# A first pair split by columns over two queues, and the first batch's natural keys of pairs 2 and 3 loaded instead of turned

## The chip, the core and the metric

The kernel runs on one core of a Trainium2 chip. The time is the device time of one execution in microseconds (us), from launch to end, median over the runs shown. The core has five engines with instruction streams of their own: PE (TensorE, matmuls), DVE (VectorE), ACT (ScalarE), POOL (GpSimd) and SP (SyncE, which here only issues transfers). Each works through its stream in order; PE alone fetches weights ahead. SP and ACT both issue direct transfers (DMAs), each on a queue of its own, and the same 16 DMA engines serve both queues.

## The reference

Inputs q, k, v are 8 batches x 8 heads x 576 positions x 64; the mixture of experts has 8 experts of 512 x 1024 x 512.

```python
scores = scale * np.matmul(q, k.transpose(0, 1, 3, 2))
rel = pos[:, None] - pos[None, :]
Dmat = np.where(rel >= 0, gamma[:, None, None] ** rel[None, :, :], 0.0)
ret = np.matmul(scores * Dmat[None], v)            # retention, no softmax
x = ret.transpose(0, 2, 1, 3).reshape(4608, 512)   # one row per token
...
expert_idx = np.argmax(logits, axis=1)             # one expert per token
h = np.maximum(x[mask] @ w1[e], 0.0)
out[mask] = gate_w[mask, None] * (h @ w2[e])
```

## The kernel before, in words

**Attention.** A batch is worked on in four pairs of heads (p = 0 to 3) and four chunks of 128 positions, with a tail of 64. For a pair the host lays q and k out turned (`qk`, head dimension on the partitions, 2 x 576 columns), k once more naturally (`kn`, positions on the partitions), and v naturally. Per batch: `emit_A` multiplies k by q within each chunk (8 matmuls per pair, each two pieces in the trace) and DVE multiplies the two result banks by the decay matrix into `raw`. `emit_U` (for the first batch `emit_U0`, two pairs at a time) multiplies natural k, scaled by a power of gamma, with v and sums over the chunks into the state `Tst`: ACT copies chunk 0, DVE adds the other three. `emit_O` adds scores times v, `emit_S` adds the state times q, `emit_At` and `emit_Ot` do the tail. The rows then go to DRAM (`xd`), and routing runs beside it. After batch 7 the mixture of experts takes from about 140 us to the end.

**The first batch** stands apart (`first_batch`), since it runs while its data arrive. `keep_warm` gives PE 38 dummy matmuls of 132 columns. Natural k of batch 0 isn't loaded: for each pair `turn_k` transposes four chunks of k on PE into one bank, and DVE scales that bank into `kt` (line 699). The order on PE: dummies, A and turn of pair 0, a small product for the experts' norms (`norm_E`), A and turn of pair 1, `emit_O(0, 0)`, `emit_U0(0)`, then A and turn of pair 2, A and turn of pair 3, `emit_S(0, 0)`, `emit_At`, `emit_U0(1)`, `emit_O(0, 1)`, `emit_S(0, 1)`, `emit_Ot`. POOL builds decay matrices and scales q. From batch 1 on POOL scales loaded k (`scale_k`, line 689). PSUM has eight banks; in the first batch `psa` hands out four in turn (a_64 to a_67 in the rows) and `psm` the other four.

**Order of the work.** All five streams are written in program order (`tc.manual_schedule`). A DMA takes one of eight semaphores (DMAHW0 to DMAHW7) in turn, over both queues together; so the ninth DMA isn't issued until the DMA that last held its semaphore has landed, and an engine that issues DMAs stands still at that point. On ACT this matters for more than DMAs: all of ACT's first transfers stand ahead of its first computation, the copy of `Tst` chunk 0 (line 775), which needs the activation table loaded just before it. Transfers of batch 0, in program order: `cs` (constants; SP), pair 0 as rows 0 to 95 of q (SP), k (ACT), rows 96 to 127 of q (ACT), pair 1 as q (SP) and k (ACT), the second constants (ACT), the first half of v (both), pairs 2 and 3 (q on SP, k on ACT), the second half of v (both), the tail constants `decayt` and `gtail` (ACT), the tail of v (SP). Then SP goes on with batch 1: four times 576 KB of `qk`, 1024 KB of `kn`, 1152 KB of v.

Of the kernel before, what the change touches and what calls it, by code (L numbers as in the profile page):

```python
# [9 lines left out]
F32 = mybir.dt.float32  # L10
# [33 lines left out]
SECOND = (0, 4, 1, 5, 2, 3, 6, 7)  # L44
BIG = 1.0e6
NWARM = 38
WWARM = 132
NO = NT + 2
NVS = 4

# [45 lines left out]
def retention_moe(ctx: ExitStack, tc: tile.TileContext, qk, kn, v0s, vs, w1, w2, head, cst, out):  # L96
# [38 lines left out]
    def cc(name):  # L135
        if name == "iota":
            return iota
        o, w = _C[name]
        return cs[:, o : o + w] if o < _FIRST else late["cd"][:, o - _FIRST : o - _FIRST + w]
# [364 lines left out]
    with ExitStack() as att:  # L504
# [16 lines left out]
            return lambda: on.tensor_tensor(out=lo, in0=raw, in1=hi.bitcast(F32), op=ALU.subtract)  # L521

        both = (nc.sync, nc.scalar)

        def load_qk(b, p):
            t = qkp.tile([P, 2, S], F32, name="qkt")
            if b == 0:
                n = 96 if p == 0 else P
                for i, on in enumerate(both):
                    m = P if i else n  # L530
                    on.dma_start(out=t[:m, i], in_=qk[b, p, :m, i])
                if n < P:
                    nc.scalar.dma_start(out=t[n:, 0], in_=qk[b, p, n:, 0])
            else:
                nc.sync.dma_start(out=t, in_=qk[b, p])
            qkt[b, p] = t
# [20 lines left out]
        def load_decay(o, w, on=nc.sync):  # L557
            on.dma_start(out=cd[:, o : o + w], in_=cst[:, o : o + w])
# [14 lines left out]
            on.dma_start(out=v0[:, c, : DM // 2], in_=v1[:, c, : DM // 2])  # L573
        load_qk(0, 2)
        load_qk(0, 3)
        for i, on in enumerate(both):
            c = slice(2 * i, 2 * i + 2)
            on.dma_start(out=v0[:, c, DM // 2 :], in_=v1[:, c, DM // 2 :])
        load_decay(0, _C["decayt"][1] + _C["gtail"][1], nc.scalar)
        nc.sync.dma_start(out=vt_[0][:, KW:], in_=v0s[:, KW:])  # L580
        kt[0] = a1.tile([P, KW], F32, name="kt", bufs=2)

        onef = ap.tile([P, P], F32, name="onef")
        part = cc("part")
# [91 lines left out]
        def kview(b):  # L676
            return kt[b].rearrange("p (c n) -> p c n", c=NCH)
# [15 lines left out]
        def turn_k(p):  # L693

            ps = psa.tile([P, 512], F32, name="a")
            for c in range(NCH):
                nc.tensor.transpose(ps[:, c * P : (c + 1) * P], qkt[0, p][:, 1, c * P : (c + 1) * P], ident)
            g = cc("gneg").rearrange("p (c h) -> p c h", c=NCH)[:, :, 2 * p : 2 * p + 2]
            nc.vector.tensor_tensor(
                out=kview(0)[:, :, p * P : (p + 1) * P].rearrange("p c (h d) -> p c h d", h=2),  # L700
                in0=ps.rearrange("p (c h d) -> p c h d", c=NCH, h=2),
                in1=g.unsqueeze(3).broadcast_to([P, NCH, 2, D]),
                op=ALU.mult,
            )

        def scale_q(b, p):
            q = qkt[b, p][:, 0, P : NCH * P]
# [232 lines left out]
        def first_batch():  # L940
            build_decay(0)
            square_E()
            emit_A(0, 0)
            turn_k(0)
            norm_E()
            build_decay(1)
            build_g(0)
            emit_A(0, 1)
            turn_k(1)
            build_decay(2)  # L950
            scale_q(0, 0)
            build_decay(3)
            build_g(1)
            scale_q(0, 1)
            build_g(2)
            build_g(3)
            emit_O(0, 0)
            emit_U0(0)
            for p in (2, 3):
                emit_A(0, p)  # L960
                turn_k(p)
                scale_q(0, p)
            emit_S(0, 0)
            emit_At(0)
            build_rest()
            emit_U0(1)
            emit_O(0, 1)
            build_E()
            scale_k(1)
            emit_S(0, 1)  # L970
            emit_Ot(0)
# [626 lines left out]
```

## Time and profile before

| | |
|---|---|
| median of 3 runs | 570.05 us (569.20 to 570.09) |
| the profiled execution's own time | 570.68 us |
| its span, first to last instruction | 568.7 us |
| PE busy | 560.5 us, 99% of the span |
| DVE, ACT, POOL busy | 420.7, 384.6, 235.2 us |
| DMA engines' mean busy share from 5 to 120 us | about 1.0 |
| chain that ended last, by engine | PE 80%, DMA 11%, waits for issue 3%, DVE 2%, ACT 2% |

A row of the timeline gives the start, the length, engine, line and operation, the tiles (output <- input) and how many were merged; in brackets the idle time before it and what ended it. A row of the chain gives the start, the length without overlap, and what the chain ran through. "L697" is line 697 of the kernel before.

### The profile page before, as it was taken

The page shows a single profiled execution, that of the slowest core. Times are in us where ns is not written, and L with a number is a line of the kernel's source. Part 1 is how long each engine was busy: PE and PEld are TensorE (multiplying, and loading weights), DVE is VectorE, ACT ScalarE, POOL GpSimd, SP SyncE. Part 2 cuts the span into 40 slices and gives each one's busy share as a digit, 9 for nine tenths or more (in the row PEclk, how much of TensorE's full clock was granted, in tenths as well). Part 3 has the DMA queues.
Part 4 walks back from the last instruction along what each step waited for, and adds up shares of the span by engine and source line. Part 5 has one row for each costly group of instructions (what it writes and reads, how often), then busy time and mean ns, then how long its engine had stood idle before and what let it go on. Part 6 is the DMA issues. An engine that isn't in the chain of part 4 may idle for free.

```text
span 568.7 us, 13084 instructions
## 1 busy us (share of the span) xinstructions
PE 560.5 (99%) x5090; PEld 508.5 (89%) x5090; DVE 420.7 (74%) x938; ACT 384.6 (68%) x700; POOL 235.2 (41%) x233
## 2 busy tenths in 40 slices
PE   8999999999999999999999999999999999999996
PEld 8898999888998899889989988998899899889986
DVE  3756768889866868877887878688778778786810
ACT  0156455457759887987787788778877877867611
POOL 6673534563446740562075126405520650242012
PEclk9999999999999999999999999999999999999999
DMA  9999999967469573557448445735564584432201
GB/s 300 406 368 373 376 342 350 389 204 242 169 207 181 180 200 116 156 160 181 124 142 196 139 117 189 182 112 168 164 150 131 158 185 143 138 99 85 75 37 50
DMA packets 74832, 109.22 MB, mean 192 GB/s; under 512 B 42344, under 2 KB 43788, under 8 KB 73872
## 3 DMA queue, kind: packets, MB, share of 16 engines
q1 hardware_dynamic: 65616, 86.17, 49.2%
q0 software_dynamic: 7696, 19.95, 10.9%
q10 hardware_dynamic: 1456, 2.24, 1.2%
q8 instruction: 41, 0.67, 0.5%
q14 instruction: 23, 0.19, 0.1%
HBM read 80.27 MB, written 19.94 MB: 176 GB/s over the span
## 4 chain that ended last, share of the span: by engine, by line
PE 80%; DMA 11%; issue 3%; DVE 2%; ACT 2%; POOL 1%; POOLq 0%; SPq 0%; DVEq 0%; ACTq 0%
PE m L1275 19%; PE a L1207 15%; PE m L1207 11%; PE a L1275 10%; DMA out<-y,sid 9%; PE a L718 4%; PE a L459 2%; PE a L801 2%; PE m L801 2%; PE m L718 2%; PE m L459 2%; PE m L884 1%; PE a L884 1%; PE m L745 1%; DMA raw<-w 1%
## 5 line engine op out<-in xcount | busy, mean ns | idle before, releaser
L1275 PE MATMUL m<-w2s,hs 128*128 128x512 f32 x600 | 138.8, 389 | 0.0
L1275 PEld LDWEIGHTS m<-w2s,hs 128*128 128x128 f32 x600 | 112.2, 188 | 22.9
L1251 POOL DMA_INDIRECT out<-y,sid x41 | 46.6, 1136 | 193.5 <-DVE wsum L1129 125.7
L1275 PE MATMUL a<-w2s,hs 128*128 128x512 f32 (+1 forms) x384 | 83.6, 376 | 0.0
L1275 PEld LDWEIGHTS a<-w2s,hs 128*128 128x128 f32 x384 | 68.9, 188 | 13.1
L1207 PE MATMUL a<-xsb,w0s 128*128 128x320 f32 x342 | 58.0, 309 | 0.0
L1207 PEld LDWEIGHTS a<-xsb,w0s 128*128 128x128 f32 x342 | 52.1, 188 | 0.0
L362 POOL DMA_INDIRECT raw<-xd,gid x40 | 43.5, 1087 | 20.3 <-DVE sid L352 7.9
L1178 ACT ACTIVATE hs<-y 128x320 fp32r<-128x320 f32 x84 | 39.3, 474 | 17.6 <-DVE y L1219 16.7
L375 POOL DMA_INDIRECT gt<-gd,gid x40 | 43.1, 1078 | 18.9 <-issue 10.5
L1171 DVE SCALAR_TENSOR_TENSOR hs<-y,hs 128x320 fp32r<-128x320 f32 x84 | 46.7, 569 | 2.0
L410 ACT COPY raw<-raw 128x1024 uint16<-128x1024 uint16 x35 | 47.4, 1355 | 0.0
L445 ACT CAST xsb<-raw 128x128 fp32r<-128x128 f32 x70 | 32.1, 459 | 21.9 <-DVE raw L428 21.4
L689 POOL TENSOR_TENSOR kt<-kt,cs 128x512 f32<-128x512 f32 x28 | 28.3, 1042 | 43.9 <-DMA kt<-kn 43.9
L1106 DVE TENSOR_TENSOR w2s<-raw,w2s 128x1024 fp32r<-128x1024 f32 x32 | 39.1, 1222 | 7.0 <-ACT w2s L1103 6.9
L1219 DVE TENSOR_TENSOR y<-a,y 128x320 f32<-128x320 f32 x47 | 22.7, 488 | 19.8 <-ACT y L1223 13.5
L403 ACT COPY raw<-raw 128x1024 uint16<-128x1024 uint16 x35 | 35.4, 1046 | 0.0
L1103 ACT CAST w2s<-raw 128x1024 fp32r<-128x1024 f32 x32 | 33.5, 1046 | 2.6 <-DMA raw<-w 2.6
L1207 PE MATMUL m<-xsb,w0s 128*128 128x320 f32 x198 | 34.1, 309 | 0.0
L708 POOL TENSOR_TENSOR qkt<-qkt,gsb 128x384 f32<-128x384 f32 x32 | 31.3, 1003 | 6.8 <-issue 4.6
L421 DVE TENSOR_TENSOR raw<-raw 128x256 f32<-128x256 f32 x35 | 14.9, 424 | 25.7 <-ACT raw L410 25.7
L1223 ACT COPY y<-a 128x320 f32<-128x320 f32 x48 | 20.5, 427 | 16.8 <-PE a L1207 12.7
(256 smaller groups left out, 1205.2 us busy)
## 6 DMA issues: line engine op xcount, KB each, us to landing
raw<-w SPq DMA_DIRECT2D x64, 512.0 KB, 3.9
qkt<-qk SPq DMA_DIRECT2D x28, 576.0 KB, 7.5
xd<-y SPq DMA_DIRECT2D x36, 256.0 KB, 9.6
vt<-vs SPq DMA_DIRECT2D x7, 1152.0 KB, 13.0
kt<-kn SPq DMA_DIRECT2D x7, 1024.0 KB, 10.4
qkt<-qk ACTq DMA_DIRECT2D x4, 288.0 KB, 5.0
qkt<-qk SPq DMA_DIRECT2D x3, 288.0 KB, 5.7
out<-y,sid POOLq DMA_INDIRECT x41, 3.2
```

Of the source, the lines that this page charges most:

```text
L362: nc.gpsimd.indirect_dma_start(out=t[:, XO : XO + DM], out_offset=None, in_=xd[:rows, :], in_offset=bass.IndirectOffsetOnAxis(ap=gid[:, a ...
L375: nc.gpsimd.indirect_dma_start(out=g[:, i : i + 1], out_offset=None, in_=gd[:, :], in_offset=bass.IndirectOffsetOnAxis(ap=gid[:, a : a + 1 ...
L403: nc.scalar.copy(far.rearrange("p (h n) -> p h n", h=2), near.rearrange("p (n h) -> p h n", h=2))
L410: nc.scalar.copy(far.bitcast(U16).rearrange("p (n h) -> p h n", h=2), near.rearrange("p (h n) -> p h n", h=2))
L718: nc.tensor.matmul(ps[h][:, c * P : (c + 1) * P], t[hs, 1, c * P : (c + 1) * P], t[hs, 0, c * P : (c + 1) * P], start=True, stop=True,)
L1103: nc.scalar.copy(hi, u)
L1106: nc.vector.tensor_tensor(out=lo, in0=u, in1=hi.bitcast(F32), op=ALU.subtract)
L1171: nc.vector.scalar_tensor_tensor(out=lo, in0=part(src), scalar=0.0, in1=hi.bitcast(F32), op0=ALU.max, op1=ALU.subtract)
L1178: nc.scalar.activation(hi, part(src), AF.Relu)
L1207: nc.tensor.matmul(ps[:, :HC], w[:, ws, ka, d * P : (d + 1) * P], xop(kx, xsp)[:, d, :], start=(n in (1, 2, 5) and d == 0 and k == 0), sto ...
L1251: put = nc.gpsimd.indirect_dma_start(out=out.rearrange("t (k n) -> (t k) n", k=k), out_offset=bass.IndirectOffsetOnAxis(ap=rows, axis=0), ...
L1275: nc.tensor.matmul(ps[:, :step], hs[:, hsp, f, i * P : (i + 1) * P], w[:, ws, f, n : n + step], start=(j == 0 and k == 0), stop=(j == NF - ...
```

## The change

- Pair 0 of batch 0 is loaded by columns instead of by rows: columns 0 to 255 of q (SP) and of k (ACT), then 256 to 511 of k (ACT), 256 to 415 of q (SP), 416 to 511 of q (ACT). Its tail columns 512 to 575 come later, in two transfers (128 partitions x 256 B each), behind the second half of v.
- `turn_k(2)` and `turn_k(3)` are gone: eight transposes on PE and two scalings on DVE. In their place natural k of pairs 2 and 3 is loaded, 256 KB on SP (chunks 0, 1) and 256 KB on ACT (chunks 2, 3), ahead of the second half of v; pair 2 is then scaled in place by eight ACT operations of 128 x 64, pair 3 by one DVE operation of 128 x 512.
- The dummy matmuls have 112 columns instead of 132.

```diff
@@ -44,7 +44,7 @@
 SECOND = (0, 4, 1, 5, 2, 3, 6, 7)
 BIG = 1.0e6
 NWARM = 38
-WWARM = 132
+WWARM = 112
 NO = NT + 2
 NVS = 4
 
@@ -521,16 +521,17 @@
             return lambda: on.tensor_tensor(out=lo, in0=raw, in1=hi.bitcast(F32), op=ALU.subtract)
 
         both = (nc.sync, nc.scalar)
+        FIRST = ((0, 0, 0, 256), (1, 1, 0, 256), (1, 1, 256, 512), (0, 0, 256, 416), (1, 0, 416, 512))
 
         def load_qk(b, p):
             t = qkp.tile([P, 2, S], F32, name="qkt")
             if b == 0:
-                n = 96 if p == 0 else P
-                for i, on in enumerate(both):
-                    m = P if i else n
-                    on.dma_start(out=t[:m, i], in_=qk[b, p, :m, i])
-                if n < P:
-                    nc.scalar.dma_start(out=t[n:, 0], in_=qk[b, p, n:, 0])
+                if p == 0:
+                    for on, i, j, k in FIRST:
+                        both[on].dma_start(out=t[:, i, j:k], in_=qk[b, p, :, i, j:k])
+                else:
+                    for i, on in enumerate(both):
+                        on.dma_start(out=t[:, i], in_=qk[b, p, :, i])
             else:
                 nc.sync.dma_start(out=t, in_=qk[b, p])
             qkt[b, p] = t
@@ -573,12 +574,18 @@
             on.dma_start(out=v0[:, c, : DM // 2], in_=v1[:, c, : DM // 2])
         load_qk(0, 2)
         load_qk(0, 3)
+        kt[0] = a1.tile([P, KW], F32, name="kt", bufs=2)
+        k0, k1 = (x.rearrange("p (c n) -> p c n", c=NCH) for x in (kt[0], kn[0]))
+        for i, on in enumerate(both):
+            c = slice(2 * i, 2 * i + 2)
+            on.dma_start(out=k0[:, c, DM // 2 :], in_=k1[:, c, DM // 2 :])
         for i, on in enumerate(both):
             c = slice(2 * i, 2 * i + 2)
             on.dma_start(out=v0[:, c, DM // 2 :], in_=v1[:, c, DM // 2 :])
+        for i, on in enumerate(both):
+            on.dma_start(out=qkt[0, 0][:, i, NCH * P :], in_=qk[0, 0, :, i, NCH * P :])
         load_decay(0, _C["decayt"][1] + _C["gtail"][1], nc.scalar)
         nc.sync.dma_start(out=vt_[0][:, KW:], in_=v0s[:, KW:])
-        kt[0] = a1.tile([P, KW], F32, name="kt", bufs=2)
 
         onef = ap.tile([P, P], F32, name="onef")
         part = cc("part")
@@ -702,6 +709,18 @@
                 in1=g.unsqueeze(3).broadcast_to([P, NCH, 2, D]),
                 op=ALU.mult,
             )
+
+        def scale_k0(p):
+            x = kview(0)[:, :, p * P : (p + 1) * P].rearrange("p c (h d) -> p c h d", h=2)
+            g = cc("gneg").rearrange("p (c h) -> p c h", c=NCH)[:, :, 2 * p : 2 * p + 2]
+            if p == 2:
+                for c in range(NCH):
+                    for h in range(2):
+                        nc.scalar.activation(x[:, c, h], x[:, c, h], AF.Copy, scale=g[:, c, h : h + 1])
+            else:
+                nc.vector.tensor_tensor(
+                    out=x, in0=x, in1=g.unsqueeze(3).broadcast_to([P, NCH, 2, D]), op=ALU.mult
+                )
 
         def scale_q(b, p):
             q = qkt[b, p][:, 0, P : NCH * P]
@@ -958,7 +977,7 @@
             emit_U0(0)
             for p in (2, 3):
                 emit_A(0, p)
-                turn_k(p)
+                scale_k0(p)
                 scale_q(0, p)
             emit_S(0, 0)
             emit_At(0)
```

Three places of the instruction streams follow, as built. Names: `qkt` is a pair's turned q and k, `cd` the constants, `vt` v, `kt` natural k; "waits DMAHW7" means that the instruction waits until the DMA that last took semaphore 7 has landed.

ACT from its fourth transfer to the work behind the first copy, before (L531 loads k of pairs 2 and 3, the last `cd` holds `decayt` and `gtail`):

```order
L558 DMA cd<-cst 128x388
L573 DMA vt<-v0s 128x2x256 [waits DMAHW1_49]
L531 DMA qkt<-qk 128x576 [waits DMAHW3_49]
L531 DMA qkt<-qk 128x576 [waits DMAHW5_49]
L578 DMA vt<-v0s 128x2x256 [waits DMAHW7_49]
L558 DMA cd<-cst 128x512 [waits DMAHW1_49]
L775 ACT_TABLE_LOAD
L775 COPY Tst<-m_68 128x128 [waits PE_49]
L827 COPY xT<-m_70 128x512 [waits PE_49]
```

The same place in the changed kernel:

```order
L574 DMA vt<-v0s 128x2x256 [waits DMAHW2_49]
L534 DMA qkt<-qk 128x576 [waits DMAHW4_49]
L534 DMA qkt<-qk 128x576 [waits DMAHW6_49]
L581 DMA kt<-kn 128x2x256 [waits DMAHW0_49]
L584 DMA vt<-v0s 128x2x256 [waits DMAHW2_49]
L586 DMA qkt<-qk 128x64 [waits DMAHW5_49]
L559 DMA cd<-cst 128x512 [waits DMAHW7_49]
L794 ACT_TABLE_LOAD
L794 COPY Tst<-m_68 128x128 [waits PE_49]
L719 ACTIVATE kt<-kt,cs 128x64 [waits DMAHW1_49]
L719 ACTIVATE kt<-kt,cs 128x64 x3
L719 ACTIVATE kt<-kt,cs 128x64 [waits DMAHW0_49]
```

Two more transfers stand ahead of the table load there, and the last `cd`, which took over semaphore 1 from the first half of v, now takes over semaphore 7.

SP from the q of pair 1 on, before and then changed (the fourth row of the second piece is the q of pair 3):

```order
L531 DMA qkt<-qk 128x576
L573 DMA vt<-v0s 128x2x256
L531 DMA qkt<-qk 128x576 [waits DMAHW0_49]
L531 DMA qkt<-qk 128x576 [waits DMAHW2_49]
L578 DMA vt<-v0s 128x2x256 [waits DMAHW4_49]
```

```order
L534 DMA qkt<-qk 128x576
L574 DMA vt<-v0s 128x2x256 [waits DMAHW1_49]
L534 DMA qkt<-qk 128x576 [waits DMAHW3_49]
L534 DMA qkt<-qk 128x576 [waits DMAHW5_49]
L581 DMA kt<-kn 128x2x256 [waits DMAHW7_49]
```

SP's half of the new `kt` has the place that its second half of v had; it takes semaphore 7 over from the q of pair 1, and ACT's last `cd` takes it over from this `kt`.

PE from the end of batch 0's tail (`emit_Ot`) to the first scores of batch 1, before and then changed:

```order
L857 MATMUL a_66<-qkt,Tst 64x64 [waits DVE_49]
L857 MATMUL a_66<-qkt,Tst 64x64
L857 MATMUL a_67<-qkt,Tst 64x64 x2
L718 MATMUL a_64<-qkt 128x128 [waits DMAHW0_49]
L718 MATMUL a_65<-qkt 128x128
```

```order
L876 MATMUL a_64<-qkt,Tst 64x64 [waits DVE_49]
L876 MATMUL a_64<-qkt,Tst 64x64
L876 MATMUL a_65<-qkt,Tst 64x64 x2
L737 MATMUL a_64<-qkt 128x128 [waits DMAHW6_49,DVE_49]
L737 MATMUL a_65<-qkt 128x128 [waits DVE_49]
```

Two banks fewer are handed out in the first batch, so batch 1's first scores now take the two banks that the tail has just written, and wait for DVE to empty them.

## Rows read from the trace of the kernel before

**Rows 1.** The page, part 1: engine, busy us (share of the span), instructions.

```profile
PE 560.5 (99%) x5090; PEld 508.5 (89%) x5090; DVE 420.7 (74%) x938; ACT 384.6 (68%) x700; POOL 235.2 (41%) x233
```

**Rows 2.** The chain of work from 0 to 120 us: start us, us, what.

```profile
1.18 4.52 DMA qkt<-qk
5.83 2.08 PE a L718 x16
...
14.10 1.09 PE a L718 x16
15.19 0.59 PE a L697 x4
...
17.20 0.58 PE a L697 x4
...
19.05 1.08 PE a L767 x32
...
23.16 0.42 PE a L718 x4
23.82 1.83 PE a L718 x28
```

**Rows 3.** Timeline of PE, 0 to 31 us.

```profile
0.75 4.34 PE L597 MATMUL m<-const-bfloat16-1.0 128*128 128x132 bf16 x38 [0.75 <-PEq L1589]
...
12.96 1.14 PE L767 MATMUL m<-vt,kt 128*64 128x64 f32 x32
...
30.70 2.08 PE L745 MATMUL m<-vt,kt 128*64 128x64 f32 x64
```

**Rows 4.** Timeline of ACT, 0 to 30 us.

```profile
9.97 0.33 ACTq L558 DMA_DIRECT2D cd<-cst  x1
10.33 1.28 ACT L775 ACT_TABLE_LOAD   x1 [10.33 <-DMA qkt<-qk]
14.15 0.27 ACT L775 COPY Tst<-m 128x128 f32<-128x128 f32 x1 [2.54 <-PE m L767]
```

**Rows 5.** Timeline of DVE, 13 to 25 us.

```profile
14.45 0.94 DVE L777 TENSOR_TENSOR Tst<-m,Tst 128x128 f32<-128x128 f32 x3 [1.82 <-ACT Tst L775]
15.31 1.28 DVE L727 TENSOR_TENSOR raw<-a,decay 128x512 f32<-128x512 f32 x2
16.51 0.68 DVE L699 TENSOR_TENSOR kt<-a,cs 128x512 f32<-128x512 f32 x1
17.11 1.28 DVE L727 TENSOR_TENSOR raw<-a,decay 128x512 f32<-128x512 f32 x2
18.31 0.68 DVE L699 TENSOR_TENSOR kt<-a,cs 128x512 f32<-128x512 f32 x1
...
23.20 0.49 DVE L868 TENSOR_TENSOR xC<-a,cd 128x128 f32<-128x128 f32 x2 [0.97 <-PE a L857]
```

**Rows 6.** Timeline of SP, 0 to 30 us: issues of q of pair 3, v, v of batch 1.

```profile
5.71 0.33 SPq L531 DMA_DIRECT2D qkt<-qk  x1
...
7.40 0.38 SPq L578 DMA_DIRECT2D vt<-v0s  x1
...
15.55 0.46 SPq L548 DMA_DIRECT2D vt<-vs  x1
```

**Rows 7.** DMA issues near 1.2, 4.7, 5.7, 7.4, 10.0, 15.5 us: KB, us to landing.

```profile
qkt<-qk SPq DMA_DIRECT2D x1, 216.0 KB, 4.5
...
vt<-v0s ACTq DMA_DIRECT2D x1, 256.0 KB, 5.2
...
qkt<-qk SPq DMA_DIRECT2D x1, 288.0 KB, 5.8
...
vt<-v0s SPq DMA_DIRECT2D x1, 256.0 KB, 6.1
...
cd<-cst ACTq DMA_DIRECT2D x1, 256.0 KB, 8.0
...
vt<-vs SPq DMA_DIRECT2D x1, 1152.0 KB, 11.9
```

**Rows 8.** Timeline of POOL, 22 us on: the scaling of batch 1's natural k.

```profile
24.46 4.05 POOL L689 TENSOR_TENSOR kt<-kt,cs 128x512 f32<-128x512 f32 x4 [4.48 <-DMA kt<-kn]
```

**Rows 9.** Groups of ACT by line: count, busy us, mean ns of one.

```profile
L830 ACT COPY xC<-a 128x64 f32<-128x64 f32 x9 | 2.1, 235 | 4.9 <-PE a L817 4.9
```

## The prediction, on record before the changed kernel ran

> **What bounds the kernel now.** I read the page first: PE is busy for 99% of the span [rows 1], so time is won only where PE starts earlier, has less to do, or waits less. The change touches the first 24 us alone, so I next read the chain of work through the attention. It begins with one wait, for the first pair (issued at 1.18 us, done at 5.70), and then runs through PE without a break to 23.58 us [rows 2]: shortening PE's list there looks like a pure gain. The third view, the timelines of the other engines in that stretch, says why it isn't. The eight transposes that go lie in front of emit_U0(1), which starts at 19.05 us [rows 2]. DVE ends the scaling that emit_U0(1) reads at 18.31 + 0.68 = 18.99 us [rows 5]. So two chains meet there within 0.06 us: PE's own list, and DVE's. The reader should follow DVE's backwards: it is busy without a break from 14.45 us, and began when ACT's first copy ended, at 14.15 + 0.27 = 14.42 us [rows 4, 5]. That copy waited 2.54 us for PE, after ACT's last transfer was issued at 9.97 us and the table load ended at 11.61 [rows 4].
>
> **The first pair earlier.** The warm-up ended at 5.09 us and PE stood until 5.83 [rows 2, 3]. With 112 columns it takes 4.34 x 112/132 = 3.68 us and ends at 4.43. The 216 KB of q, behind the constants, landed 4.5 us after issue [rows 7]; now 128 KB are enough. I take a start near 5.0, a gain of 0.8 us (bounds 0 and 5.83 - 4.43 = 1.4). It ends where PE next waits.
>
> **Transposes removed.** Those of pairs 2 and 3 held 0.59 + 0.58 = 1.17 us of the chain [rows 2]. With the start, PE would come to emit_U0(1) 2.0 us earlier, were it alone.
>
> **The wait that the change adds.** ACT's last transfer (the tail constants) used to wait for the first half of v, issued at 4.74 us on ACT and landing 5.2 us later, at 9.94 [rows 7]; it was issued at 9.97 [rows 4]. It now takes semaphore 7 from SP's half of the new natural k, and ACT stands still until that has landed. Behind it on ACT wait the table load and the copy of Tst, for the copy DVE's additions, for these, in DVE's order, the scores of pairs 2 and 3, and for these the scaling of pair 3 that emit_U0(1) needs.
>
> When does that half land? Its price is not in the trace, but a twin is: in SP's order it stands where the second half of v stood, with the same 256 KB, released by the same landing of pair 1's q. The twin was issued at 7.40 us [rows 6] and took 6.1 us [rows 7], so 13.5. On SP about as many bytes lie ahead as before (1677 KB with it, against 1685). Lower bound: it cannot land before the q of pair 3, ahead of it on the same queue: 5.71 + 5.8 = 11.5 us [rows 6, 7]. Upper bound: the slowest 256 KB of that stretch took 8.0 us [rows 7], which gives 15.4. I take the twin, 13.5.
>
> Then, on ACT: issue 0.33, table load 1.28, copy 0.27 [rows 4], with 0.04 between: the copy ends at 15.42 us, 1.00 later than before. PE's earlier start doesn't help, for emit_U0(0), which the copy reads, ended at 12.96 + 1.14 = 14.1 before [rows 3] and will be done before 13.4.
>
> **DVE's chain from there.** Before, 18.99 - 14.42 = 4.57 us from the copy to the last scaling. One scaling (16.51 to 17.11, 0.60) moves to ACT; the other stays, read from SBUF instead of PSUM, and I keep its 0.68 [rows 5]. So 3.97 us: DVE ends at 19.39, emit_U0(1) runs from 19.45, **0.40 us later** than before. What hides the eight ACT operations is this chain: at 235 ns [rows 9] they take 1.9 us and end at 17.3, two us ahead of need. With the cover gone, emit_U0(1) would wait for them instead, from 15.42 + 1.9.
>
> **The bank.** Batch 1's first scores ran at 23.16 us [rows 2], beside DVE's emptying of the tail's banks (23.20 + 0.49 = 23.69 [rows 5]). Now they wait for it: a start at 23.75. Four pieces went before the pause that ended at 23.82 [rows 2]; at full pace (16 in 1.09 us) they take 0.27, so the rest follows at 24.02 instead of 23.82: **+0.20**, and up to 23.75 + 0.42 + 0.24 - 23.82 = 0.59 if that pause comes again.
>
> **More to transfer.** The DMA engines are full here, and 512 KB are added. The v of batch 1 landed at 15.55 + 11.9 = 27.45 us [rows 6, 7] and is wanted at 30.70 [rows 3]: 3.25 us to spare. Its natural k is scaled chunk by chunk until 28.51 [rows 8], and the last chunk is wanted some 1.5 us into that product: 3.7 to spare. The transfers of batches 0 and 1 up to that v are some 8.5 MB in 27.45 us, so 512 KB cost some 1.7 us; gaps in the queue may cost 1 more. Both fit, and PE comes later, not earlier; I cost this at nothing. The tail constants took 8.0 us [rows 7]; from an issue at 13.5 they land by 21.5 at the latest, and their reader on DVE, ahead of the additions for emit_S(0, 1), could then cost up to some 0.7 us; behind fewer bytes than before on ACT I expect them by 20 and take nothing.
>
> **Sum.** The gains of 0.8 and 1.17 us end in waits on PE ahead of emit_U0(1). What is left is +0.40 + 0.20 = +0.60 us. From there on the chain is PE's and the shift is carried to the end. The profiled execution took 570.68 us, 0.63 above the median of 570.05; against the median the sum is **570.65 us**. With the bounds of the landing (11.5 and 15.4 for 13.5) and of the bank it runs from 568.7 to 572.9.
>
> **Rivals.**
> *Transfers come early (faster).* If the half lands near its lower bound, ACT's copy is bound by the transfers that end with pair 3: 11.5 + 0.33 (the tail's issue, which waits for the same q) + 0.33 + 1.28 + 0.27 = 13.7 us, 0.7 earlier than before. Then 0.7 + 0.6 - 0.2 = 1.1 us are won: 568.95. For it: the first transfers are smaller. Against it: the twin, and that SP's first half of v, issued at 2.12 us before, must now wait for the constants, so that the queues start less full. It decides below a landing of 12.9, where the sum crosses zero.
>
> *The clock falls (slower).* The dummies take 4.34/38 = 114 ns for 132 columns, and the first scores 2.08 us where later ones take 1.09 [rows 2, 3]: PE is at the 1.2 GHz level there, after 0.74 us of rest and light work, and at 2.4 GHz later, though the profile's clock column reads 1.0 throughout. Before, PE never rests from 5.83 to 23.58. In the changed kernel it would rest three times between 15.2 and 19.4 us (for the copy, for a bank, and 1.7 us for DVE), some 2.7 us of 4.2. If the clock falls there, emit_U0(1) (1.08 us [rows 2]) and what follows it run at half pace and lose as much time as they take at full pace; the scores and transposes of pair 0 lost about 1 + 0.5 us in that way at the start [rows 2]. I take 1.4 us, with the sum 572.05. Against it: no row of before shows a fall once the clock is up. The Trainium skill speaks against this change here: TensorE: Matmul & The Clock Gate, Part 1, has the half rate as the default to which an engine left idle returns, and says that any work issued before the release runs at 1.2 GHz. No run so far shows that return; by that rule, if the rest counts as idle, the time is this rival's.
>
> *The half, or the tail constants, come late (slower).* A landing near 14.5 instead of 13.5 adds 1.0, the constants up to 0.7: 571.3 to 572.3, say 571.7.
>
> *The first pair isn't earlier.* Then 0.8 us less of rest, and the same end, since ACT's copy waits for the transfer either way; it is inside the forecast.
>
> **How the numbers follow.** A difference of 0.2% (1.14 us) is about what a measurement of this kernel can tell from no change. The forecast (570.1 to 571.2) gets 0.55, the early transfers 0.18, the fallen clock 0.12, the late half 0.15. Faster by more than 0.2% (below 568.9): rather less than half of the early case, and some for noise and for shifts later on: 0.13. Slower by more (above 571.2): the clock, nearly all of the late case, and an edge of the forecast: 0.29. The rest is 0.58. The range leaves out a tenth at either end: 568.7 to 572.2.
>
> **What would show it.** In the changed profile: PE's first scores near 5.0 us; ACT's last transfer issued near 13.5 us instead of 9.97, its table load right behind, and the copy of Tst ending near 15.4; DVE's additions starting right then; PE resting ahead of emit_U0(1), which starts near 19.4; batch 1's first scores waiting for DVE near 24. I am wrong if that last transfer is issued before 12.9 us, if the copy waits for PE again, if the matmuls behind 19.4 us run at twice their length, or if a product of batch 1 waits for v or k.

## The result, and the profile after

The change takes **573.7 us** (median of 6 runs, 573.22 to 574.4), the kernel before 570.07 beside it (6 runs). The ratio is 1.0057, 95% interval [1.0035, 1.0078]: slower by 3.6 us, 1.5 us above the top of the range. The profiled execution took 573.85 us with a span of 572.0.

PE's work fell as its list says, by eight instructions and about 2 us of busy time (page, part 1, for [rows 1]):

```profile
PE 558.3 (98%) x5082; PEld 506.3 (89%) x5082; DVE 419.2 (73%) x937; ACT 385.8 (67%) x708; POOL 236.6 (41%) x233
```

So the loss is waiting. PE's timeline from 0 to 33 us (start us, us, engine, line, operation, and in brackets the idle time ahead of it with what ended it), for [rows 2, 3]:

```profile
0.75 3.43 PE L604 MATMUL m<-const-bfloat16-1.0 128*128 128x112 bf16 x38 [0.75 <-PEq L1608]
4.26 0.71 PE L737 MATMUL a<-qkt 64*128 64x128 f32 x8
6.76 0.93 PE L737 MATMUL a<-qkt 64*128 64x128 f32 x8 [1.79 <-DMA qkt<-qk]
...
8.90 1.92 PE L737 MATMUL a<-qkt 64*128 64x128 f32 x16
...
13.15 1.14 PE L786 MATMUL m<-vt,kt 128*64 128x64 f32 x32
...
17.92 0.68 PE L859 MATMUL a<-qkt 64*64 64x64 f32 x16 [0.83 <-DMA qkt<-qk]
...
19.91 1.03 PE L786 MATMUL a<-vt,kt 128*64 128x64 f32 x28 [1.04 <-DVE kt L721]
...
24.35 2.13 PE L737 MATMUL a<-qkt 64*128 64x128 f32 x31 [0.38 <-DVE xC L887]
...
31.64 1.56 PE L764 MATMUL m<-vt,kt 128*64 128x64 f32 x46
```

The first half of pair 0 starts at 4.26 us. The second half isn't there: PE rests 1.79 us, and the pair as a whole is ready at 6.76, where it was ready at 5.83 before. What follows is slow (16 scores take 1.92 us), so emit_U0(0) (13.15) is no earlier than before. Further down PE rests 0.83 us for the first pair's tail columns, 1.04 us for DVE (emit_U0(1) gets going at 19.91) and 0.38 us for a bank at batch 1's first scores. ACT in the same stretch, for [rows 4]:

```profile
12.11 0.35 ACTq L586 DMA_DIRECT2D qkt<-qk  x1
13.95 0.35 ACTq L559 DMA_DIRECT2D cd<-cst  x1
14.33 1.28 ACT L794 ACT_TABLE_LOAD   x1 [14.33 <-DMA kt<-kn]
15.62 0.27 ACT L794 COPY Tst<-m 128x128 f32<-128x128 f32 x1
```

This is the wait that was forecast: the tail's issue ends at 12.46 us, ACT stands until 13.95, issues its last transfer, loads its table, and copies Tst from 15.62 to 15.89. In the chain of waits (start us, us, what) the transfer behind it is SP's half of the natural k:

```profile
7.70 6.23 DMA kt<-kn
```

It landed at 13.93. DVE, for [rows 5], follows the copy at once and ends the scaling that emit_U0(1) reads at 19.17 + 0.68 = 19.85 us:

```profile
15.92 0.94 DVE L796 TENSOR_TENSOR Tst<-m,Tst 128x128 f32<-128x128 f32 x3 [3.10 <-ACT Tst L794]
16.78 2.47 DVE L746 TENSOR_TENSOR raw<-a,decay 128x512 f32<-128x512 f32 x4
19.17 0.68 DVE L721 TENSOR_TENSOR kt<-kt,cs 128x512 f32<-128x512 f32 x1
```

The table by stretches (the stretch and its length in us, busy us of PE, PEld, DVE, ACT and POOL, then the granted clock, the DMA share and GB/s) shows what was slow on PE:

```profile
6.00:8.00 2.00, 1.24 (x10) 1.04 (x11) 0.26 (x1) 0.00 (x0) 0.72 (x1) 0.78 0.98 345
8.00:10.00 2.00, 2.00 (x16) 1.98 (x16) 1.70 (x4) 0.00 (x0) 1.56 (x4) 0.50 1.07 400
10.00:12.00 2.00, 2.00 (x26) 1.71 (x26) 1.07 (x2) 0.00 (x0) 2.00 (x4) 0.87 1.04 380
12.00:14.00 2.00, 2.00 (x54) 2.00 (x51) 0.81 (x2) 0.00 (x0) 1.90 (x4) 1.00 1.12 352
...
18.00:20.00 2.00, 0.96 (x22) 0.75 (x24) 2.00 (x5) 0.75 (x2) 2.00 (x2) 1.00 1.00 354
```

The granted clock is 0.50 between 8 and 10 us, PE's 1.2 GHz level, behind the rest between the pair's halves. It is back at 1.00 from 12 us on, and stays there through the rests of 16 to 20 us.

### The profile page after: what moved, and what is told of

It reads as the page before. It is cut to its first block, busy times and chain, and to the rows that moved or that the text cites. A ratio compares the mean times of both kernels' runs of the same rounds, so it can differ in the third digit from the quotient of the medians.

```text
span 572.0 us, 13089 instructions
## 1 busy us (share of the span) xinstructions
PE 558.3 (98%) x5082; PEld 506.3 (89%) x5082; DVE 419.2 (73%) x937; ACT 385.8 (67%) x708; POOL 236.6 (41%) x233
## 4 chain that ended last, share of the span: by engine, by line
PE 78%; DMA 13%; issue 3%; ACT 3%; DVE 2%; POOL 1%; SPq 0%; POOLq 0%; ACTq 0%
PE m L1294 19%; PE a L1226 15%; PE m L1226 11%; PE a L1294 10%; DMA out<-y,sid 9%; PE a L459 2%; PE m L737 2%; PE a L820 2%; PE a L737 2%; PE m L459 2%; PE m L820 2%; PE m L903 1%; PE a L903 1%; PE m L764 1%; DMA kt<-kn 1%
```

## The experiments

Seventeen runs followed, two of them the two kernels again, each beside the kernel before on the same chip; ratios are against that. A ratio is not the quotient of the two medians and differs from it by up to 0.0017. The table gives what their traces show of the first batch (us): the start of the copy of Tst on ACT, the start of emit_U0(1) (of its last 28 products where they come in two groups), the start of batch 1's products with state (L745 before, L764 in the change).

| kernel | copy | emit_U0(1) | batch 1 | median | ratio [95%] |
|---|---|---|---|---|---|
| before, first profile | 14.15 | 18.98 | 30.70 | 570.07 | |
| r_before | 12.87 | 17.70 | 29.69 | 570.85 | 1.0008 [0.9982, 1.0033] |
| e_align | 12.57 | 17.40 | 29.32 | 570.18 | 0.9994 [0.9980, 1.0008] |
| e_load | 12.39 | 17.22 | 29.20 | 569.80 | 1.0010 [0.9989, 1.0030] |
| the change | 15.62 | 19.91 | 31.64 | 573.70 | 1.0057 [1.0035, 1.0078] |
| r_after | 15.80 | 20.08 | 31.86 | 574.00 | 1.0063 [1.0043, 1.0083] |
| a_align | 15.77 | 20.06 | 31.86 | 574.47 | 1.0087 [1.0072, 1.0103] |
| e_act | 15.65 | 19.93 | 31.67 | 571.63 | 1.0027 [1.0009, 1.0046] |
| e_split | 14.25 | 19.08 | 30.89 | 571.75 | 1.0030 [1.0013, 1.0048] |
| e_keys | 14.38 | 18.84 | 30.63 | 570.53 | 1.0012 [1.0000, 1.0024] |
| e_delay | 12.85 | 20.14 | 31.35 | 572.92 | 1.0050 [1.0033, 1.0066] |
| a_warm | 15.59 | 19.87 | 32.95 | 574.61 | 1.0082 [1.0061, 1.0104] |
| a_both | 13.57 | 18.36 | 31.68 | 571.35 | 1.0013 [1.0000, 1.0026] |
| a_four | 16.54 | 20.82 | 32.55 | 572.35 | 1.0034 [1.0019, 1.0048] |
| a_tail | 13.49 | 17.51 | 30.12 | 570.75 | 1.0019 [1.0005, 1.0032] |
| e_split_warm | 13.61 | 18.45 | 31.08 | 571.03 | 1.0024 [1.0013, 1.0035] |
| a_best | 13.91 | 18.77 | 31.53 | 571.64 | 1.0030 [1.0012, 1.0048] |
| a_sp | 13.07 | 18.13 | 33.09 | 570.90 | 1.0008 [0.9988, 1.0028] |
| k_sp | 13.89 | 18.82 | 30.55 | 569.86 | 0.9994 [0.9975, 1.0014] |

The start of emit_U0(1) in the first profile is that of PE's timeline; the chain of waits in [rows 2] has 19.05.

A row shows one execution, the median several; where they seem to differ (e_act, a_four, a_both, a_sp) the profile shows a late first batch. In a_align and e_delay it is the other way round: the profiled execution is the fastest of its six (571.06 and 570.88 us), late as its first batch is.

### Both kernels again

r_before and r_after are the two kernels unchanged.

> The kernel before, unchanged, once more with its profile. PE's waits with no releaser shown ('issue') between 20 and 150 us sum to 0.96 us in the first profile of before and 2.57 us in that of the change. Theory F (instruction fetch: where these waits fall is set by the program): they return at the same places, near 55 us, 0.8 us. Theory C (chance): they fall elsewhere, and their sum may be anything between 1 and 3 us. Ratio 1.000.

> The change, unchanged, once more with its profile. Both: 573.7 us, ratio 1.006; the batch-1 scores 0.5 us and batch 1's first U product 0.95 us later than before. Theory F: the four issue waits (near 56.7, 83, 89.4 and 122.4 us) return at the same instructions. Theory C: at least two of them are gone or stand elsewhere.

The times repeat. The profile of before doesn't. PE's timeline of r_before:

```profile
5.94 1.16 PE L718 MATMUL a<-qkt 64*128 64x128 f32 x16 [0.86 <-DMA qkt<-qk]
...
11.73 1.10 PE L767 MATMUL m<-vt,kt 128*64 128x64 f32 x32
...
17.70 1.15 PE L767 MATMUL a<-vt,kt 128*64 128x64 f32 x32
...
29.69 2.08 PE L745 MATMUL m<-vt,kt 128*64 128x64 f32 x64
```

The same 16 first scores take 1.16 us here and took 2.08 in the profile that the prediction was made from [rows 2], and what follows is 1.0 to 1.3 us earlier in r_before: emit_U0(0) at 11.73 for 12.96 [rows 3]. e_load and e_align show the 1.16 us too. ACT in r_before:

```profile
10.34 0.34 ACTq L558 DMA_DIRECT2D cd<-cst  x1
...
12.87 0.27 ACT L775 COPY Tst<-m 128x128 f32<-128x128 f32 x1 [0.88 <-PE m L767]
```

The copy is at 12.87 and waits for PE. So in three of four executions with the first batch of before emit_U0(1) starts at 17.2 to 17.7 us, and in the three of the change at 19.9 to 20.1: means of 17.44 and 20.02, **2.58 us**. At batch 1's products with state 2.39 us are left (29.40 against 31.79).

### Added bytes, and the place of the instructions

e_load adds to the kernel before the 512 KB alone, into a buffer that is not in use yet, ahead of batch 1's transfers:

```diff
+        nc.sync.dma_start(out=raws[3][:, : KW // 2], in_=kn[0, :, : KW // 2])
```

> The kernel before, with one transfer of 512 KB more on SP, behind v's tail and ahead of batch 1, into a buffer that nothing reads before it is written again; PE's stream is the same. Theory D (the added bytes put every later transfer and instruction fetch of the attention 1.5 us further back, and PE pays in issue waits): the first 23 us as before, but 1.5 to 2.4 us more by the end, 572. Theory of the prediction (the slack hides it): 570.1, ratio 1.000.

569.80 us, 1.0010 [0.9989, 1.0030]: the bytes themselves, behind the first batch's own transfers, cost nothing that can be measured.

e_align (before: `NWARM, WWARM = 30, 167`) and a_align (the change: 46, 93) move PE's list by whole instructions.

> The kernel before, with 30 dummy matmuls of 167 columns instead of 38 of 132: the same warm-up time, but PE's stream is 16 instructions shorter, as in the change. Theory F: PE's issue waits move to emit_S of batches 4 and 6, as in all profiles of the change, and the time rises by about 1 us: 571.2. Rival (these waits follow from how late PE and the transfers are): no stall there, 570.2, ratio 1.000.

> The change, with 46 dummy matmuls of 93 columns instead of 38 of 112: PE's stream is as long as before again from pair 0 on. Theory F: the stalls in emit_S of batches 4 and 6 go, 573. Rival: they stay, 574.

By the places of the pauses that the trace puts down to "issue", theory F holds in part: r_after repeats three of the change's four; e_align has one in emit_U at 80.75 us and one in emit_S at 86.88, where the change has them at 82.97 and 89.42; a_align has neither. By the time it falls: neither median moved toward the other kernel's. The one traced execution of a_align, without these two pauses, was however 3.2 us faster than the next of its six, so what they cost is not settled.

### The change in two parts

e_split has the split, the tails sent late and the shorter warm-up; the four turns stay. e_keys has the natural keys alone (the parts of the diff on `kt[0]` and `scale_k0`).

> One half of the change alone: pair 0 by columns, its tail columns late, 112-column dummies; all four turns stay. ACT's last transfer waits for pair 3's q here, not for a natural k. Theory S (the split is what hurts: PE starts on the first columns near 4.3 us, then rests until the rest lands near 6.7, later than the whole pair did, and its clock falls to the half rate until about 12 us): emit_U0(0) starts at 13 us or later, 571 to 572. Rival (ACT's wait is the whole loss of the first batch, the split wins 0.8 us as predicted): emit_U0(0) near 12, 569.3.

> The other half alone: natural k of pairs 2 and 3 loaded and scaled, two turns gone; pair 0 by rows and 132-column dummies as before. ACT's last transfer takes its semaphore from pair 2's k here (about 11.3 us), so ACT's copy waits for PE again. Theory S: the first batch ends 0.2 to 0.6 us earlier than in the profile of before, and by the first batch alone 569.8. Rival K (loading and scaling the keys costs by itself: late data for emit_U0(1), or the bank): emit_U0(1) no earlier than 19 us, 571. Theory F (PE's stream is 16 instructions shorter, and its waits for issue move into the products of batches 4 and 6): on top of either 1 us, with stalls in emit_S of batches 4 and 6.

+0.30% and +0.12%, together less than the 0.57 to 0.63% of the change, though the intervals leave room for a plain sum. Neither part gains.

### ACT's last transfer

e_act sends it on SP:

```diff
-        load_decay(0, _C["decayt"][1] + _C["gtail"][1], nc.scalar)
         nc.sync.dma_start(out=vt_[0][:, KW:], in_=v0s[:, KW:])
+        load_decay(0, _C["decayt"][1] + _C["gtail"][1])
```

> The change, with the last transfer of ACT (the tail constants) moved to SP behind v's tail; nothing else. Theory A (ACT's wait for the new natural k is what the first batch loses): ACT's copy of Tst ends near 14.4 us instead of 15.9, emit_U0(1) starts near 18.4 instead of 19.9, and 1.0 to 1.5 us come back: 572.3. Rival (PE waits for pair 0's tail columns and for data just the same): emit_U0(1) not before 19.4, time 573.4.

571.63 beside 574.00 for r_after: 2.4 us come back by the medians, 2.1 by the ratios. The traced execution (572.83 us) doesn't show how. ACT has its table loaded by 13.70 us there, but the first scores ran slow (8 take 1.23 us, for 0.71 in the change), and the copy waits for PE; emit_U0(1) is at 19.93 and not near 18.4. PE and ACT in e_act:

```profile
4.38 1.23 PE L737 MATMUL a<-qkt 64*128 64x128 f32 x8
...
12.42 1.28 ACT L794 ACT_TABLE_LOAD   x1 [12.42 <-DMA qkt<-qk]
15.65 0.27 ACT L794 COPY Tst<-m 128x128 f32<-128x128 f32 x1 [1.95 <-PE m L786]
```

a_tail leaves the transfer on ACT and makes the list of transfers one shorter, by sending the first pair's two tails together on SP. ACT's last transfer then takes over semaphore 5 instead of 7, from the q of pair 3, which SP issues directly ahead of the natural k.

```diff
-        for i, on in enumerate(both):
-            on.dma_start(out=qkt[0, 0][:, i, NCH * P :], in_=qk[0, 0, :, i, NCH * P :])
+        nc.sync.dma_start(out=qkt[0, 0][:, :, NCH * P :], in_=qk[0, 0, :, :, NCH * P :])
```

> The change with the first pair's two tails (32 KB each) in one transfer on SP instead of one on each queue. The bytes and TensorE's work stay; with one transfer fewer, ACT's last one takes the semaphore ahead, that of SP's half of pair 3 (issued about 6.5), in place of that of the natural k's half (issued 7.7, landed 13.9). Theory A (it is which transfer this semaphore belongs to): ACT issues its last transfer by 12.1, the copy of Tst is near 13.6 to 15 and the time is near that with the transfer on SP (571.63): 571.2 to 572.2, ratio 1.0020 to 1.0040. If the semaphore isn't it (if it was the transfer's place on ACT or its bytes): 573.2 to 574.4, ratio 1.0055 or more.

570.75 us, 1.0019 [1.0005, 1.0032]: the same bytes, the same work on PE, and by the ratios 0.44% less than r_after, 2.5 us. ACT in a_tail:

```profile
11.82 0.35 ACTq L559 DMA_DIRECT2D cd<-cst  x1
12.19 1.28 ACT L793 ACT_TABLE_LOAD   x1 [12.19 <-DMA qkt<-qk]
13.49 0.27 ACT L793 COPY Tst<-m 128x128 f32<-128x128 f32 x1
```

The last transfer goes out at 11.82 us, what ended the wait ahead of the table load is a `qkt` and no longer the natural k, and the copy is 2.1 us earlier than in the change. This shows that the wait is that for a reused semaphore, set by how many transfers stand ahead. What is late next stands in PE's timeline of a_tail:

```profile
6.17 0.71 PE L736 MATMUL a<-qkt 64*128 64x128 f32 x8 [1.24 <-DMA qkt<-qk]
...
16.90 0.68 PE L858 MATMUL a<-qkt 64*64 64x64 f32 x16 [1.00 <-DMA qkt<-qk]
17.51 1.35 PE L785 MATMUL a<-vt,kt 128*64 128x64 f32 x32
...
30.12 2.09 PE L763 MATMUL m<-vt,kt 128*64 128x64 f32 x64
```

The tail columns, sent behind v as in the change, make PE wait until 16.90.

### The shift alone

e_delay puts ten idle products of 512 columns ahead of the first batch's tail scores in the kernel before, into a bank that these scores overwrite.

```diff
+        wide = nc.const_aps.tensor_like(1.0, like=a2.tile([P, 512], BF16, name="junk", bufs=1))
...
+            if b == 0:
+                for _ in range(10):
+                    nc.tensor.matmul(ps, one, wide, start=True, stop=True)
```

> The kernel before, with ten more products of 512 bf16 columns ahead of the first batch's tail scores (512 columns at 2.4 GHz are 0.213 us each, 2.13 us in all; nothing else changes, no transfer and no wait). It copies the change's shift at batch 1's U products (about +2.0 us: four runs of kernels that keep the four turns started them at 29.2 to 30.7, four that have the change at 31.6 to 31.9) without any of the change's causes. Theory O (one shift, carried one to one): about 570.2 + 2.1 = 572.3 us, ratio near 1.0037; U products of batch 1 near 31.8, mixture products near 174.7. Theory M (a later start makes later batches lose more, about 1 us as in the change): about 573.4, ratio 1.0057 or more, mixture products at 175.7 or later. If the first batch has slack that takes it in: under 571.0.

PE's timeline of e_delay, the added products (nine of the ten are in the trace) and emit_U0(1):

```profile
17.23 2.36 PE L839 MATMUL a<-const-bfloat16-1.0 128*128 128x512 bf16 x9
...
20.14 1.15 PE L769 MATMUL a<-vt,kt 128*64 128x64 f32 x32
```

emit_U0(1) starts at 20.14 us, as late as in the change, with no transfer and no wait changed. The time is 572.92, 1.0050 [1.0033, 1.0066], +2.6 us by the medians: a late first batch alone costs what the change costs, within the intervals, and is carried to the end. Whether it grows a little on the way (theory M) stays open: the interval holds 1.0037 and 1.0057. That is so for the six executions together. In the traced one batch 1's products with state are 1.95 us late (31.35 against the 29.40 above), and the mixture's first products with the second layer's weights 0.98 (173.42 against a mean of 172.44 in the same three executions of before); these three spread from 171.62 to 173.08, so a single execution says little here.

### The clock

a_warm lengthens the warm-up of the change so that PE doesn't rest between the pair's halves; a_both does that and sends ACT's last transfer on SP.

```diff
-WWARM = 112
+WWARM = 180
```

> The change, with 180 columns instead of 112 in each of the 38 products that warm TensorE, so that it doesn't rest between the first pair's two halves: the warm-up ends near 6 us, the second half has landed by 6.6. Granted clock from 6 to 12 us: 1.00 in each stretch of 2 us (it was 0.78 to 0.92, 0.50, 0.73 to 0.87). Theory A (ACT's wait alone sets the shift): the copy of Tst still starts at 15.5 or later behind the last transfer on ACT, so 573.2 to 574.0, ratio 1.0055 to 1.007. Theory S (the clock's fall costs its own part): U products of batch 1 start about 1 us earlier than 31.7, and the time is 572.4 to 573.0, ratio 1.004 to 1.005.

> The change with the longer warm-up (180 columns) and with the last transfer of the tail constants on SP's queue instead of ACT's: both suspected causes away, the split and the loaded natural keys stay. If those two are the whole cause: 570.0 to 570.8, ratio 0.9995 to 1.0012, U products of batch 1 at 29.5 to 30.5. If something else of the change costs (the added waits for products' banks, the order of the transfers, the code's length): 571.2 or more, ratio 1.002 or more. With the last transfer on SP alone it was 571.63.

PE's timeline of a_warm, the first scores, emit_U0(0) and emit_U0(1):

```profile
6.17 1.16 PE L737 MATMUL a<-qkt 64*128 64x128 f32 x16
...
11.73 1.10 PE L786 MATMUL m<-vt,kt 128*64 128x64 f32 x32
...
19.87 1.76 PE L786 MATMUL a<-vt,kt 128*64 128x64 f32 x28 [1.41 <-DVE kt L721]
```

Its table by stretches (columns as above):

```profile
8.00:10.00 2.00, 2.00 (x23) 1.71 (x24) 2.00 (x6) 0.00 (x0) 1.55 (x3) 1.00 1.06 398
...
18.00:20.00 2.00, 0.59 (x12) 0.38 (x10) 2.00 (x5) 0.72 (x2) 2.00 (x2) 0.84 1.01 410
20.00:22.00 2.00, 2.00 (x34) 2.00 (x36) 0.74 (x9) 0.27 (x1) 0.27 (x1) 0.50 1.06 434
22.00:24.00 2.00, 2.00 (x34) 1.83 (x33) 1.59 (x9) 0.00 (x0) 0.00 (x0) 0.81 0.98 399
```

The clock is 1.00 up to 18 us and emit_U0(0) starts at 11.73, 1.4 us earlier than in the change, and nothing is won: 574.61 us. The copy still waits for ACT's last transfer, at 15.59. PE only rests longer (1.18, 0.47 and 1.41 us ahead of emit_U0(1)), and in this execution the clock falls behind that rest, to 0.50 between 20 and 22 us; 28 products that took 1.03 us take 1.76. a_both, with neither the wait nor the fall, has 571.35, 1.0013 [1.0000, 1.0026].

e_split_warm is the split alone with the same long warm-up.

> The split alone (the four turns stay, no natural k is loaded), with 180 columns instead of 112 in each of the 38 warm-up products. The split alone was 571.75, ratio 1.0030 [1.0013, 1.0048], with a granted clock of 0.53 and 0.62 between 8 and 12 us. Theory S (there the clock's fall is the cost, since nothing later than TensorE is waited for): clock 1.00 throughout, 570.0 to 570.8, ratio 0.9995 to 1.001. If the later landing of the first pair's second half (6.6 against 5.9) costs by itself: 571.0 to 572.0, ratio 1.0015 or more.

1.0024 [1.0013, 1.0035], for 1.0030 without it, and a granted clock of 1.00 throughout: the fall isn't the cost of the split either, or only a small part. Its copy of Tst is at 13.61 behind ACT's last transfer (issued at 11.95; 10.34 in r_before).

### Four pieces, and versions meant to win

a_four has four pieces of 256 columns instead of five; a_best has these, the joined tails and 180 columns.

```diff
-        FIRST = ((0, 0, 0, 256), (1, 1, 0, 256), (1, 1, 256, 512), (0, 0, 256, 416), (1, 0, 416, 512))
+        FIRST = ((0, 0, 0, 256), (1, 1, 0, 256), (0, 0, 256, 512), (1, 1, 256, 512))
```

> The change with the first pair in four pieces of 256 columns, q on SP and k on ACT, so that no row of a piece is shorter than 1 KB and each queue carries the same. If the pieces of 80 KB and 48 KB were late for their short rows (4.4 to 5.0 us from issue to landing against 2.6 to 2.9 for those of 128 KB): the second half's scores start near 6.0 instead of 6.6 to 6.8, the clock may stay at 1.00, and the time is up to 0.7 us lower, 573.0 to 573.6. If they were late for all that is in flight by then: the second half's scores stay at 6.5 to 6.9 and the time at 573.5 to 574.3. The order on both queues behind it doesn't move, so ACT's wait stays.

> Everything of the change that the runs speak against taken out, its two aims kept: four pieces of 256 columns, the two tails in one transfer on SP, 180 columns in each warm-up product; ACT's last transfer then takes the semaphore of a transfer that lands before 10 us. If the two waits were all: 570.0 to 571.0, ratio 0.9995 to 1.0015, no better than the kernel before, since the natural k (512 KB more ahead of batch 0's end) lands near 14 to 15 and its scaling on ACT stands where the turns' did. If the turns saved are worth their 1.17 us of TensorE once the waits are gone: 569.0 or less, ratio 0.998 or less. If the added bytes ahead of the first batch's end cost by themselves: 571.2 or more.

The second half came no earlier, but at 7.51 and 7.75 us: short rows were not why it is late. a_four is yet 1.4 us below the change, and below both expectations. Its list is one transfer shorter, as a_tail's, and ACT's last transfer goes out at 13.02 us instead of 13.95; but in the traced execution the copy waits for PE until 16.54, so that this is the reason is not shown. a_best is slower than before, 1.0030 [1.0012, 1.0048]: PE waits until 7.75 for the second half and until 18.16 for the tails.

a_sp is a_tail with ACT's last transfer on SP and the tails sent ahead of the natural k. k_sp is e_keys with that transfer on SP, without the split.

> The change with the last transfer of the tail constants on SP (ACT then issues nothing behind its half of v) and the first pair's two tails in one transfer on SP ahead of the natural k instead of behind v. In the kernel before, ACT could copy Tst as soon as TensorE was done, at 12.87; in the change it copied at 15.6, with one transfer fewer at 13.5, and there the tail's scores waited for the tail columns until 16.9. If these two waits are what is left (theory A carried through): copy at 12.9, no wait for the tail, U0(1) near 17.2, 569.3 to 570.2, ratio 0.998 to 1.0005. If the natural k, scaled on ACT at 14.6 or later, is late next: U0(1) at 17.5 to 18.5, 570.3 to 571.0, ratio 1.0005 to 1.002. If the later second half costs by itself, as in the split alone with the long warm-up (1.0024): 571 or more.

> The natural keys alone (the first pair as before, by partitions, with its tails, and 132 columns of warm-up), with the last transfer of the tail constants on SP. The keys alone were 570.53, ratio 1.0012 [1.0000, 1.0024], with the copy of Tst at 14.38 behind ACT's last transfer. If that wait was their cost: the copy at 12.9 to 13.3, U0(1) near 17, and with the 1.17 us of turns gone 568.8 to 569.8, ratio 0.9975 to 0.9995, below both kernels. If the natural k's landing (14 to 15, for 512 KB more on full queues) is late next: no better than before, 569.8 to 570.5, ratio 0.9995 to 1.001.

Neither can be told from the kernel before: 1.0008 [0.9988, 1.0028] and 0.9994 [0.9975, 1.0014]. With ACT's wait gone the 1.17 us of transposes are still not won in the traced execution of k_sp; its interval by itself would leave room for them (a gain of 1.17 us is a ratio of 0.9979). ACT's timeline in k_sp:

```profile
9.94 0.39 ACTq L582 DMA_DIRECT2D vt<-v0s  x1
...
13.89 0.27 ACT L790 COPY Tst<-m 128x128 f32<-128x128 f32 x1 [2.25 <-PE m L782]
```

The copy waits for PE alone, as before. PE's timeline in k_sp, the first scores and emit_U0(1):

```profile
5.88 2.08 PE L733 MATMUL a<-qkt 64*128 64x128 f32 x16 [0.80 <-DMA qkt<-qk]
...
18.82 1.03 PE L782 MATMUL a<-vt,kt 128*64 128x64 f32 x28 [1.46 <-DVE kt L717]
```

emit_U0(1) waits 1.46 us for DVE, whose last scaling in k_sp is this row of its timeline:

```profile
17.45 1.32 DVE L717 TENSOR_TENSOR kt<-kt,cs 128x512 f32<-128x512 f32 x1
```

From the copy to that scaling's end DVE's chain lasts 18.77 - 14.16 = 4.61 us, as long as the 4.57 of before. One scaling has left it, and the other takes 1.32 us for 0.68 (0.73 in a_tail, 1.46 in a_sp). Why that one is longer in some executions stays open.

## Why the prediction was wrong

**The wait that the change adds: mechanism right, landing 0.4 to 0.6 us late.** The half landed at 13.93 instead of 13.5, ACT's last transfer was issued at 13.95 (14.13 in r_after, 14.10 in a_align), the copy ended at 15.89 instead of 15.42.

**DVE's chain from there: the term that failed.** The chain came out as worked: DVE's end at 19.85 for 19.39, emit_U0(1) at 19.91 for 19.45. What was wrong is what it was subtracted from. The sum put 19.45 against 19.05 in the one profiled execution, +0.40, and there PE was itself late: its first scores ran at 2.08 us, and the copy waited for PE until 14.15. In the three other executions the copy is at 12.4 to 12.9 and emit_U0(1) at 17.2 to 17.7. Against these the copy is 3.1 us later and not 1.00, and the term is **+2.6 us instead of +0.40**. Of the 2.18 us between the two, 1.61 come from the profile subtracted from (19.05 for 17.44) and 0.57 from the later landing (20.02 for 19.45). The prediction had the sign in hand: its rival on the clock says that those scores ran at half pace, and it took this for the rule. That the profiled execution's time was only 0.63 us above the median did not warn of it.

**The first pair earlier: wrong, and without effect in the change.** One half started at 4.26, but the second could not before 6.2 to 7.8 us in all kernels with a split, so the pair is later than before, not 0.8 earlier. The step took the first 128 KB for the whole. The rival for this gave the same end, since ACT waits either way; a_warm shows that. Without that wait the split has a cost of its own: 0.24 to 0.30% in e_split_warm and e_split.

**Transposes removed: right.** They end in a wait.

**The bank: the wait is there** (0.38 us, [rows 5] answer to it), **but costs nothing net**: from emit_U0(1) to batch 1 there are 11.73 us in the change, 11.99 in r_before, 11.72 in the first profile. In the place of the wait these two have a pause of 0.51 and 0.23 us put down to "issue".

**More to transfer: right.** No product of batch 1 waited for v or k, and e_load shows no cost that can be measured.

**The shift is carried to the end: right on the median**, by e_delay. Of the 3.6 us, 2.4 to 2.6 are seen in the first batch; the rest, some 1 us, lies in pauses put down to "issue" that differ from run to run by as much, and the intervals don't tell whether it belongs to the change.

**The clock falls: it did, elsewhere.** In the change it fell behind the rest between the pair's halves (0.50 at 8 to 10 us), not at 15 to 19, and ACT's wait covered it. At the rival's place it fell in a_warm. The Trainium skill, TensorE: Matmul & The Clock Gate, Part 1, has the engine return to the half rate when idle; these two granted clocks of 0.50 agree, but the change's rests of 0.83 and 1.04 us from 17 to 20 us brought no fall.

The other rivals: the transfer was not early, and 0.4 to 0.6 us late, which is the 0.57 above. The tail constants made no product wait: DVE's reader of them started at 19.79 in the change without a wait, and in r_after at 20.60 behind one of 0.57, with no wait of PE behind it.

## What to carry to other kernels

One transfer more or less on a list that shares its completion semaphores changes which earlier transfer each later issue waits for; where that issue stands on an engine that also computes, follow what is behind it. A time difference is taken between two executions of the usual kind: before a term rests on a profile of before, look whether its rows run at their usual length, in a second profile or against their twins in the same one. Where two chains meet at one instruction, work taken off one of them is worth nothing until the other is shorter too.

## What the chip showed that was not expected

The first scores ran at 2.08 us in some executions of one order and at 1.16 in others, and the granted clock reads 1.00 in both. k_sp's stretch from 6 to 8 us, inside such a slow start:

```profile
6.00:8.00 2.00, 2.00 (x17) 1.77 (x18) 0.16 (x1) 0.00 (x0) 1.92 (x4) 1.00 1.07 377
```

The same stretch in r_before:

```profile
6.00:8.00 2.00, 2.00 (x25) 1.86 (x26) 1.13 (x5) 0.00 (x0) 1.92 (x4) 1.00 1.07 375
```

PE issues 17 instructions in k_sp where it issues 25 in r_before. A start like that makes the first batch 1 us late. Of the seven traced executions that start in the order of before, two have it (before and k_sp), so a median may hold both kinds; how many of each isn't known. What sets the kind stays open. Second, PE's rest between the first pair's halves brought the clock down in some kernels only: behind 1.79 us in the change it read 0.50, behind 1.24 us in a_tail and 1.21 us in a_sp 1.00. The length of the rest alone doesn't decide it: e_split fell to 0.53 behind 1.20 us, and a_best stayed at 1.00 behind 1.48.
